# Block spectra of a long convolution: r's tiles ahead of u's, and x, v and decoded weights in other places

## The chip, the cores and the metric

The kernel runs on one core of one Trainium2 chip. The metric is the device time of one execution in microseconds.

## The reference

The inputs x and v are 12480 x 128, the positions 12480 x 64; everything is float32. A small network makes a filter from the positions, a long convolution mixes u = x * v with it, and two two-layer networks follow:

```
h_filt = (relu(pos_emb @ w1) @ w2) * exp(-0.01 * pos)
y = irfft(rfft(x * v, n=2*S) * rfft(h_filt, n=2*S))[:S]        # along the sequence, S = 12480
a = x * y
h = a @ w_in;  g = where(h > 0, h, exp(min(h, 0)) - 1);  b = g @ w_out          # d_ff = 2048
h = b @ w_in2; out = (max(h, 0) + alpha * min(h, 0)) @ w_out2
```

The weights of the two networks arrive with their 32-bit words interleaved in pairs as 64-bit numbers; the kernel decodes each of the four matrices into a rounded part (hi) and a remainder (lo).

## The kernel before

The Fourier transforms are block transforms, written as matrix products. The program is written out by hand in order: within an engine the order of the code is the order of the instructions, and engines wait for one another by semaphores. There are four stages.

The first makes r = relu(pos_emb @ w1): eight groups (`r_group`) of eight matmuls each, evicted from PSUM by ScalarE (one half) and VectorE (the other) into `rreg`, a buffer of 8192 columns per partition. Positions are loaded into the first 6272 columns of `ureg` (`load_pos`).

The second stage, the block spectra, has 48 tiles of four matmuls (`a_tile`), each into one of four PSUM buffers `pa` of two banks. The 16 r tiles (kind 1) multiply columns of `rreg` with `fw_sb` and are evicted into `sa` and `sb`; the 32 u tiles (kind 0) multiply u = x * v with `f_sb` and are evicted into `ureg`, which they fill altogether. ScalarE evicts the real half of each tile; VectorE evicts the other half in two tiles of three, ScalarE in the third. `order` lists two u tiles, then one r tile, sixteen times. `load_u` loads x and v of one u tile (98 partitions x 512 columns each, 0.40 MB for the pair) from SyncE's queue into a pool with five buffers for x and three for v; `mul_u` multiplies them, on GpSimd or on VectorE, into the buffer of x.

Beside this the weights are decoded. A piece is 512 columns of one matrix: `dec_load(j)` loads it (0.52 MB), and `dec_op(j, i)` is one of ten steps: 1 is ScalarE's absolute value, 2 to 6 are five VectorE operations (lines 112 to 120), 7 is ScalarE's cast to hi, 8 and 9 are GpSimd's subtraction and addition that make lo, and 10 writes hi and lo to memory (`wd`) for a later reload. Each piece needs a place of 2048 columns (`fixed`). `hooks` holds the steps that are issued after tile t. Pieces 0 to 2 are decoded in the r stage, 3 to 8 in the block spectra, 9 to 15 in the third stage. Pieces 0 to 2 are written from GpSimd's queue, 3 to 8 from ScalarE's, later ones from SyncE's; a queue's issue stands in the order of its engine's instructions.

The third stage is the spectrum loop over d = 0 to 24 (`b_r`, `b_u`, `b_h`, `products`, `z_mm`): products of the two spectra, with sums on GpSimd (lines 372 to 384), and their second transform, written to memory. b_r(0) starts when all tiles are evicted; its ScalarE copies go to `rt`, columns 7168 to 7680 of `rreg`. At its end `idle_mm` issues matmuls whose result nobody reads. The fourth stage is the two networks.

In an order listing DMAHWn and DMASWn are semaphores that count transfers issued by SyncE and ScalarE and by GpSimd; Pool, DVE, Activation and PE with a number are those of the engines.

Of the kernel before, what the change touches and what calls it, by code (L numbers as in the profile page):

```python
# [18 lines left out]
D = 128  # L19
P = 64  # L20
# [20 lines left out]
def kernel(ctx: ExitStack, tc: tile.TileContext, posT, w1b, w2b, sc2, xva, xT,  # L41
# [38 lines left out]
    ups = pb.enter_context(pool("ups", 4, side="right"))  # L80
# [15 lines left out]
    def dec_op(j, i):  # L96
# [26 lines left out]
        elif i == 8:  # L123
            nc.gpsimd.tensor_tensor(bf, bf, hi, ALU.subtract)
        elif i == 9:
            nc.gpsimd.tensor_tensor(lo, bf, a, ALU.add)
        elif nm in wd:
            (nc.gpsimd if j < 3 else nc.scalar if j < 9 else nc.sync).dma_start(wd[nm][:, :, k * 512 : (k + 1) * 512], rest.rearrange("p (x w) -> p x w", x=2))
# [24 lines left out]
    NU = D // 4  # L153

    def load_u(k, t=(0, 1)):
        for c in t:
            if k < NU:
                u_raw[k, c] = ups.tile([NI, 4, 2, P], F32, name="xv"[c], bufs=(5, 3)[c])
                nc.sync.dma_start(u_raw[k, c].rearrange("i c a p -> i (c a p)"),
                                  xva[:, c, 4 * k : 4 * k + 4].rearrange("i c a p -> i (c a p)"))  # L160

    def mul_u(k, eng=nc.gpsimd):
        u_done[k] = u_raw.pop((k, 0))
        eng.tensor_tensor(u_done[k], u_done[k], u_raw.pop((k, 1)), ALU.mult)
# [20 lines left out]
    w1_sb = col(NG * GW + 4096, 128)  # L185
# [4 lines left out]
    for j in range(3):  # L190
        fixed[j] = halves(col(NG * GW + 2048 * j, 2048) if j < 2 else dreg)
    dec_load(0)
    load_pos(2, 2)
    dec_load(1)
    load_pos(4, 2)
    nc.sync.dma_start(f_sb, fmat)
    load_u(0)
    load_pos(6, 2)
    load_u(1)
    load_pos(8, 2)  # L200
    dec_load(2)
    load_pos(10, 2)
    load_u(2)
    load_pos(12, 2)
    load_pos(14, 2)
    load_u(3)
    load_u(4)
    nc.sync.dma_start(fw_sb[:NI, : 2 * NF], fwin)
    nc.sync.dma_start(w2_sb, w2b)
    load_u(5, (1,))  # L210
    hooks = {3: [(mul_u, (0,))], 4: [(mul_u, (1,))], 6: [(mul_u, (2, nc.vector))]}
    for j, s in enumerate((0, 1, 4)):
# [6 lines left out]
    mul_u(3, nc.vector)  # L219

# [22 lines left out]
    order = []  # L243
    for k in range(CC // 4):
        order += [(0, 2 * k), (0, 2 * k + 1), (1, k)]
    order = order[:-3] + [order[-1]] + order[-3:-1]

    rfree = [halves(rreg[:, 2048 * x : 2048 * x + 2048]) for x in range(2)]
    fixed.update({9: rfree[1], 3: halves(dreg), 4: rfree[0], 5: halves(dreg), 6: rfree[1], 7: rfree[0], 8: halves(dreg)})
# [610 lines left out]
```

## Time and profile before

| | us |
|---|---|
| median of 3 runs | 1418.32 (1416.62 to 1419.56) |
| the profiled execution | 1418.37 |
| its span | 1416.6 |
| TensorE busy | 1376.6 |
| VectorE busy | 1267.7 |
| ScalarE busy | 1080.5 |
| GpSimd busy | 946.0 |

The profile is one execution. Its times count from the start of the span; 1.8 us of the execution's own time lie around the span. TensorE is PE, VectorE DVE, ScalarE ACT, GpSimd POOL, SyncE SP; the queue of an engine has a q behind its name.

### The profile page before, as it was taken

Reading aid. Unit: us, or ns where it says so; the run is one execution under the profiler, and the core shown is the slowest. Engines: PE = TensorE matmul, PEld = TensorE weight load, DVE = VectorE, ACT = ScalarE, POOL = GpSimd, SP = SyncE. Lnnn points to the kernel's source line nnn. Section 1 sums busy time; section 2 is a strip of 40 time slices with the busy share of each in tenths; the row PEclk is TensorE's granted clock in tenths of the full one; section 3 lists DMA queues with packets and bytes.
Section 4 is the critical chain, followed back from the end, with each engine's and each line's share of the span. In section 5 each row is a group of like instructions: output and inputs, shape, how many; then the busy total and the mean of one; then the engine's idle time right before and its main releaser. Section 6 shows DMA issues by size and latency. Waiting matters only on the chain.

```text
span 1416.6 us, 27103 instructions
## 1 busy us (share of the span) xinstructions
PE 1376.6 (97%) x10133; PEld 1171.5 (83%) x10133; DVE 1267.7 (89%) x1782; ACT 1080.5 (76%) x2041; POOL 946.0 (67%) x840
## 2 busy tenths in 40 slices
PE   6978999899999999999999999999999999999998
PEld 6977777688888888888888888888888888888897
DVE  5677999899999999999999999999999999999997
ACT  3545676588888788888888888887888888888884
POOL 4575788666666666666676666766667666666666
PEclk9999999999999999999999999999999999999999
DMA  8785776830010000000005000000000000000000
GB/s 268 229 256 174 215 236 195 234 106 25 29 55 26 27 26 8 19 26 26 19 8 209 26 26 19 8 26 26 25 19 8 26 26 26 19 8 23 8 8 14
DMA packets 56923, 97.61 MB, mean 69 GB/s; under 512 B 4506, under 2 KB 37432, under 8 KB 55366
## 3 DMA queue, kind: packets, MB, share of 16 engines
q1 hardware_dynamic: 53276, 84.75, 19.8%
q0 software_dynamic: 1568, 7.90, 1.9%
q10 hardware_dynamic: 1947, 3.22, 0.6%
q8 instruction: 80, 1.31, 0.4%
q14 instruction: 52, 0.43, 0.1%
HBM read 70.13 MB, written 25.66 MB: 68 GB/s over the span
## 4 chain that ended last, share of the span: by engine, by line
PE 86%; DVE 6%; DMA 3%; issue 2%; ACT 1%; POOL 1%; SPq 0%; POOLq 0%; ACTq 0%; DVEq 0%
PE psh L587 13%; PE pso L588 13%; PE psh L588 13%; PE pso L589 13%; PE pso L587 13%; PE psh L589 12%; PE psi L486 3%; PE pa L225 3%; DMA x<-in_xva_dram 2%; DVE spreg L355 2%; DMA ureg<-in_posT_dram 1%; PE pu L327 1%; PE pzz L393 1%; PE prh L337 1%; PE prh L307 1%
## 5 line engine op out<-in xcount | busy, mean ns | idle before, releaser
L610 POOL TENSOR_TENSOR g1l<-ureg,g1h 128x486 fp32r<-128x486 f32 (+3 forms) x313 | 364.3, 1164 | 201.7 <-ACT g1h L636 197.9
L610 POOL TENSOR_TENSOR g2l<-ureg,g2h 128x490 fp32r<-128x490 f32 (+3 forms) x315 | 346.4, 1100 | 121.6 <-ACT g2h L659 45.7
L648 DVE TENSOR_SCALAR ureg<-psh,al_sb 128x486 f32<-128x486 f32 (+3 forms) x416 | 296.0, 712 | 53.3 <-PE psh L589 52.9
L622 ACT ACTIVATE ureg<-psh 128x490 f32<-128x490 f32 (+2 forms) x393 | 225.9, 575 | 90.4 <-PE psh L589 87.3
L653 DVE SCALAR_TENSOR_TENSOR ureg<-psh,ureg 128x486 f32<-128x486 f32 (+3 forms) x416 | 274.1, 659 | 14.3
L630 DVE SCALAR_TENSOR_TENSOR ureg<-ureg,psh 128x486 f32<-128x486 f32 (+3 forms) x416 | 268.4, 645 | 4.2 <-ACT ureg L623 2.6
L636 ACT CAST g1h<-ureg 128x490 fp32r<-128x490 f32 (+3 forms) x405 | 240.0, 593 | 19.5 <-DVE ureg L630 18.6
L623 ACT ACTIVATE ureg<-ureg 128x490 f32<-128x490 f32 (+2 forms) x393 | 239.8, 610 | 12.5
L659 ACT CAST g2h<-ureg 128x490 fp32r<-128x490 f32 (+3 forms) x404 | 234.8, 581 | 8.7 <-DVE ureg L653 6.4
L587 PE MATMUL psh<-sb,sa 128*128 128x486 f32 (+3 forms) x416 | 160.8, 386 | 0.2 <-ACT sb L490 0.2
L588 PE MATMUL psh<-sb,sa 128*128 128x486 f32 (+3 forms) x416 | 158.9, 382 | 1.2 <-DVE sb L491 1.2
L587 PE MATMUL psh<-x2h,sb 128*128 128x486 f32 (+3 forms) x416 | 158.6, 381 | 1.1 <-ACT x2h L679 1.1
L588 PE MATMUL psh<-x2l,sb 128*128 128x486 f32 (+3 forms) x416 | 158.7, 382 | 0.4 <-DVE x2l L680 0.4
L589 PE MATMUL psh<-x2h,wc 128*128 128x486 f32 (+3 forms) x416 | 158.3, 381 | 0.0
L589 PE MATMUL psh<-sb,sa 128*128 128x486 f32 (+3 forms) x416 | 157.3, 378 | 0.0
L588 PE MATMUL pso<-g1l,sa 128*128 128x490 f32 (+3 forms) x405 | 155.4, 384 | 0.7 <-POOL g1l L610 0.4
L588 PE MATMUL pso<-g2l,wc 128*128 128x490 f32 (+3 forms) x404 | 155.5, 385 | 0.5 <-POOL g2l L610 0.5
L589 PE MATMUL pso<-g2h,wc 128*128 128x490 f32 (+3 forms) x404 | 154.9, 383 | 0.0
L587 PE MATMUL pso<-g1h,sa 128*128 128x490 f32 (+3 forms) x405 | 154.4, 381 | 0.0
L589 PE MATMUL pso<-g1h,sb 128*128 128x490 f32 (+3 forms) x405 | 154.4, 381 | 0.0
L587 PE MATMUL pso<-g2h,wc 128*128 128x490 f32 (+3 forms) x404 | 154.2, 382 | 0.0
L610 DVE TENSOR_TENSOR g1l<-ureg,g1h 128x490 fp32r<-128x490 f32 (+3 forms) x104 | 122.2, 1175 | 14.6 <-ACT g1h L636 3.7
(135 smaller groups left out, 2383.6 us busy)
## 6 DMA issues: line engine op xcount, KB each, us to landing
rreg<-in_gmat_dram SPq DMA_DIRECT2D x24, 384.0 KB
ureg<-in_finv_dram SPq DMA_DIRECT2D x24, 379.0 KB
ureg<-zhi SPq DMA_DIRECT2D x4, 1584.0 KB
x<-in_xva_dram SPq DMA_DIRECT2D x32, 196.0 KB
v<-in_xva_dram SPq DMA_DIRECT2D x32, 196.0 KB
zlo<-rreg SPq DMA_DIRECT2D x24, 256.0 KB
zhi<-rreg SPq DMA_DIRECT2D x22, 256.0 KB
ureg<-zlo SPq DMA_DIRECT2D x2, 1980.0 KB
```

Source lines behind the costliest of these rows:

```text
L225: nc.tensor.matmul(ps[:, 256 * e : 256 * e + 2 * NF], src[:, c0 + e].rearrange("i a p -> i (a p)"), fm, start=True, stop=True)
L587: nc.tensor.matmul(ps[:, :w], ah, bh[:, :w], start=start, stop=False)
L588: nc.tensor.matmul(ps[:, :w], ah, bl[:, :w], start=False, stop=False)
L589: nc.tensor.matmul(ps[:, :w], al, bh[:, :w], start=False, stop=stop)
L610: eng.tensor_tensor(lo[:, :w], e[:, :w], hi[:, :w], ALU.subtract)
L622: nc.scalar.activation(e[:, :w], ps[:, :w], AF.Relu, scale=-1.0)
L623: nc.scalar.activation(e[:, :w], e[:, :w], AF.Exp, scale=-1.0)
L630: nc.vector.scalar_tensor_tensor(e[:, :w], e[:, :w], -1.0, ps[:, :w], op0=ALU.add, op1=ALU.max)
L636: nc.scalar.copy(hi[:, :w], e[:, :w])
L648: nc.vector.tensor_scalar(e[:, :w], ps[:, :w], 0.0, al_sb[:, c : c + 1], op0=ALU.min, op1=ALU.mult)
L653: nc.vector.scalar_tensor_tensor(e[:, :w], ps[:, :w], 0.0, e[:, :w], op0=ALU.max, op1=ALU.add)
L659: nc.scalar.copy(hi[:, :w], e[:, :w])
```

## The change

The 16 r tiles come first and the 32 u tiles after them. The pool for x and v becomes a list of places: eight of 512 columns in a new buffer `ring`, and, once r tile k is multiplied, column block k of `rreg`, except blocks 4 to 7 and 11 to 14, which serve as places for pieces 6, 9 and 8. A v place comes free with its product, an x place with its tile. `load_u` loads as many pairs as there are places; in the r stage two pairs are loaded one at a time between pieces, and one after w2, and the positions come ahead of most other loads. Pieces 0 to 3 and 5 are decoded in columns of `ureg` behind the positions; pieces 2, 3, 5 and 4 move so that loads come in the r stage and steps from tile 2, 4, 7 and 12 on. Writes of pieces 3 to 8 are issued from GpSimd. A quarter of the products is on VectorE. In the spectrum loop two idle matmuls go, and the last two steps of piece 15 move from behind the loop into it.

```diff
@@ -77,7 +77,7 @@
     f_sb = fpool.tile([NI, 2 * NF], F32, name="f_sb")
     dreg = fpool.tile([128, 2048], F32, name="dreg")
     sc_sb = fpool.tile([128, 1], F32, name="sc_sb")
-    ups = pb.enter_context(pool("ups", 4, side="right"))
+    ring = fpool.tile([128, 4096], F32, name="ring")
     psa = pb.enter_context(pool("psa", 4, space=PSUM))
 
 
@@ -125,7 +125,7 @@
         elif i == 9:
             nc.gpsimd.tensor_tensor(lo, bf, a, ALU.add)
         elif nm in wd:
-            (nc.gpsimd if j < 3 else nc.scalar if j < 9 else nc.sync).dma_start(wd[nm][:, :, k * 512 : (k + 1) * 512], rest.rearrange("p (x w) -> p x w", x=2))
+            (nc.gpsimd if j < 9 else nc.sync).dma_start(wd[nm][:, :, k * 512 : (k + 1) * 512], rest.rearrange("p (x w) -> p x w", x=2))
 
     DV = (9,)
     pieces = [(src, nm, k) for src, nm in ((wo2, "wo2"), (wi2, "wi2"), (wo1, "wo1"), (wi1, "wi1")) for k in range(4)]
@@ -151,17 +151,27 @@
 
     u_raw, u_done = {}, {}
     NU = D // 4
-
-    def load_u(k, t=(0, 1)):
-        for c in t:
-            if k < NU:
-                u_raw[k, c] = ups.tile([NI, 4, 2, P], F32, name="xv"[c], bufs=(5, 3)[c])
-                nc.sync.dma_start(u_raw[k, c].rearrange("i c a p -> i (c a p)"),
-                                  xva[:, c, 4 * k : 4 * k + 4].rearrange("i c a p -> i (c a p)"))
+    free = [(ring[:, 512 * x : 512 * x + 512], False) for x in range(8)]
+    nload = [0]
+
+    def load_u(most=99):
+        while most and len(free) >= 2 and nload[0] < NU:
+            k = nload[0]
+            for c in range(2):
+                u_raw[k, c] = free.pop(0)
+                nc.sync.dma_start(u_raw[k, c][0][:NI], xva[:, c, 4 * k : 4 * k + 4].rearrange("i c a p -> i (c a p)"))
+            nload[0] += 1
+            most -= 1
+
+    def release(place):
+        if not (place[1] and nload[0] > NU - 10):
+            free.append(place)
 
     def mul_u(k, eng=nc.gpsimd):
-        u_done[k] = u_raw.pop((k, 0))
-        eng.tensor_tensor(u_done[k], u_done[k], u_raw.pop((k, 1)), ALU.mult)
+        x, v = u_raw.pop((k, 0)), u_raw.pop((k, 1))
+        eng.tensor_tensor(x[0][:NI], x[0][:NI], v[0][:NI], ALU.mult)
+        release(v)
+        u_done[k] = x
 
     NG = P // PH
     GW = PH * NI
@@ -182,42 +192,42 @@
             else:
                 nc.scalar.activation(dst, src, AF.Relu)
 
-    w1_sb = col(NG * GW + 4096, 128)
+    w1_sb = col(NF * 2 * D - 128, 128)
     nc.scalar.dma_start(w1_sb, w1b)
     load_pos(0)
     nc.scalar.dma_start(sc_sb, sc2)
     load_pos(1)
-    for j in range(3):
-        fixed[j] = halves(col(NG * GW + 2048 * j, 2048) if j < 2 else dreg)
+    rfree = rreg[:, 2048:4096]
+    fixed.update({j: halves(col(NG * GW + 2048 * j, 2048)) for j in range(4)})
+    fixed.update({4: halves(dreg), 5: halves(col(NG * GW + 8192, 2048)), 6: halves(rfree), 7: halves(dreg), 8: halves(rreg[:, 5632:7680]), 9: halves(rfree)})
+    load_pos(2, 2)
     dec_load(0)
-    load_pos(2, 2)
+    load_pos(4, 2)
+    load_pos(6, 2)
     dec_load(1)
-    load_pos(4, 2)
-    nc.sync.dma_start(f_sb, fmat)
-    load_u(0)
-    load_pos(6, 2)
-    load_u(1)
     load_pos(8, 2)
-    dec_load(2)
     load_pos(10, 2)
-    load_u(2)
     load_pos(12, 2)
     load_pos(14, 2)
-    load_u(3)
-    load_u(4)
     nc.sync.dma_start(fw_sb[:NI, : 2 * NF], fwin)
+    dec_load(2)
+    load_u(1)
+    dec_load(3)
+    nc.sync.dma_start(f_sb, fmat)
+    load_u(1)
+    dec_load(5)
     nc.sync.dma_start(w2_sb, w2b)
-    load_u(5, (1,))
-    hooks = {3: [(mul_u, (0,))], 4: [(mul_u, (1,))], 6: [(mul_u, (2, nc.vector))]}
-    for j, s in enumerate((0, 1, 4)):
+    load_u(1)
+    dec_load(4)
+    load_u()
+    hooks = {}
+    for j, s in enumerate((1, 4)):
         for i, d in enumerate((0, 0, 0, 0, 0, 0, 1, 1, 1, 2), 1):
             hooks.setdefault(s + d, []).append((dec_op, (j, i)))
     for g in range(NG // 2):
         run_hooks(hooks, g)
         r_group(g)
     run_hooks(hooks, 99)
-    mul_u(3, nc.vector)
-
 
     def a_tile(src, c0, fm, dsts, d0, shared, scale=None, cuts=(0, NF)):
         ps = psa.tile([128, 1024], F32, name="pa")
@@ -240,15 +250,16 @@
                 else:
                     nc.scalar.activation(o, x, AF.Copy, scale=scale)
 
-    order = []
-    for k in range(CC // 4):
-        order += [(0, 2 * k), (0, 2 * k + 1), (1, k)]
-    order = order[:-3] + [order[-1]] + order[-3:-1]
-
-    rfree = [halves(rreg[:, 2048 * x : 2048 * x + 2048]) for x in range(2)]
-    fixed.update({9: rfree[1], 3: halves(dreg), 4: rfree[0], 5: halves(dreg), 6: rfree[1], 7: rfree[0], 8: halves(dreg)})
-    hooks = dec_plan({3: 1, 4: 12, 5: 17, 6: 24, 7: 28, 8: 33}, (4, 5, 5, 6, 7, 7, 9, 10, 12, 14))
-    hooks.setdefault(40, []).append((dec_load, (9,)))
+    order = [(1, k) for k in range(CC // 4)] + [(0, k) for k in range(NU)]
+    hooks = {}
+    for j, load, s in ((2, None, 2), (3, None, 4), (5, None, 7), (4, None, 12), (6, 14, 19), (7, 22, 27), (8, 28, 33), (9, 40, None)):
+        if load is not None:
+            hooks.setdefault(load, []).append((dec_load, (j,)))
+        if s is not None:
+            for i, d in enumerate((0, 1, 1, 2, 3, 3, 5, 6, 7, 8), 1):
+                hooks.setdefault(s + d, []).append((dec_op, (j, i)))
+    for k in range(NU):
+        hooks.setdefault((5, 7, 9, 10)[k] if k < 4 else (13 if k % 4 == 3 else 11) + k, []).append((mul_u, (k, nc.vector if k % 4 == 3 else nc.gpsimd)))
     gts = {}
 
     def load_g(d):
@@ -260,15 +271,17 @@
     for t, (kind, k) in enumerate(order):
         if kind:
             a_tile(r_sb, 4 * k, fw_sb[:NI, : 2 * NF], a_rs, 4 * k, t % 3 != 0, scale=sc_sb, cuts=(0, NR, NF))
-            if k == 11 or k == 13:
-                load_g(k // 13)
+            if not (3 < k < 8 or 10 < k < 15):
+                free.append((rreg[:, 512 * k : 512 * k + 512], 7 < k < 11))
         else:
-            a_tile(u_done.pop(k), 0, f_sb, [a_u], 4 * k, t % 3 != 0, cuts=(0, 8, NF) if t == len(order) - 1 else (0, NF))
-            load_u(k + 5, (0,))
-            if 0 < k < NU - 3:
-                mul_u(k + 3, nc.vector if k % 6 == 2 else nc.gpsimd)
-            load_u(k + 6, (1,))
+            x = u_done.pop(k)
+            a_tile(x[0][:NI].rearrange("i (c a p) -> i c a p", c=4, a=2), 0, f_sb, [a_u], 4 * k, t % 3 != 0, cuts=(0, 8, NF) if t == len(order) - 1 else (0, NF))
+            release(x)
         run_hooks(hooks, t)
+        load_u()
+        if t == len(order) - 6:
+            load_g(0)
+    load_g(1)
     run_hooks(hooks, 99)
     nc.sync.dma_start(fw_sb, wmat)
     pb.close()
@@ -507,7 +520,7 @@
         when(s, dec_load, j)
         for i, d in ((2, 2), (3, 2), (4, 3), (5, 3), (6, 4)):
             mid.setdefault(t + d, []).append((j, i))
-        for i, d in ((1, 1), (7, 6), (8, 6), (9, 6), (10, 7))[: 5 if pieces[j][1] in wd else 2 if j == 15 else 4]:
+        for i, d in ((1, 1), (7, 6 - j // 15), (8, 6 - j // 15), (9, 6), (10, 7))[: 5 if pieces[j][1] in wd else 4]:
             when(t + d, dec_op, j, i)
     when(22, z_rows, 0, 80, 0, QA)
     when(24, z_rows, 80, 88, 0, QA)
@@ -549,11 +562,8 @@
     sums(nc.vector, nc.vector)
     writes.append(z_mm(ND - 3, (1,)))
     products(*late[1])(nc.gpsimd, nc.vector)
-    for i in (8, 9):
-        dec_op(15, i)
     idle_mm(pzz, FULL)
     writes.append(z_mm(ND - 2, (1,), prh))
-    idle_mm(pzz, FULL[:2])
     inv2(0)
     writes.append(z_mm(ND - 1, (1,), prh, 256))
     for write in writes:
```

On ScalarE, at the first u tile (`ureg<-pa`), before:

```order
L183 ACTIVATE rreg<-pa 98x2x64x4 [waits PE_49]
L122 CAST dreg<-dreg 128x512 [waits DVE_49]
L183 ACTIVATE rreg<-pa 98x2x64x4 [waits PE_49] x3
L239 COPY ureg<-pa 128x99x4 [waits DMAHW1_49,DMAHW0_49,DMAHW3_49,DMASW1_49,DMAHW4_49,DMASW0_49,DMAHW5_49,PE_49,DMAHW6_49,Activation_49,Pool_49]
L239 COPY ureg<-pa 128x99x4
L239 COPY ureg<-pa 128x99x4 [waits PE_49]
```

and in the changed kernel, where DMASW0 to DMASW4 count the writes of pieces 0, 1, 2, 3 and 5:

```order
L251 ACTIVATE sb<-pa,sc_sb 128x49x4
L251 ACTIVATE sa<-pa,sc_sb 128x50x4
L251 ACTIVATE sb<-pa,sc_sb 128x49x4
L249 COPY ureg<-pa 128x99x4 [waits DMASW3_49,DMASW4_49,DMASW2_49,DMAHW2_49,DMASW1_49,DMAHW3_49,DMASW0_49,DMAHW4_49,PE_49,DMAHW7_49,Activation_49,Pool_49]
L249 COPY ureg<-pa 128x99x4 [waits PE_49]
L122 CAST dreg<-dreg 128x512 [waits DVE_49]
L249 COPY ureg<-pa 128x99x4 [waits PE_49]
```

The first copy of a u tile stood behind the last r group and waited for two writes; now it stands behind the 16 r tiles, waits for five, and the cast of piece 4 (`dreg`) stands behind it.

On GpSimd, in the same stretch, before (`x<-x,v` is a product, `wd` a write to memory):

```order
L164 TENSOR_TENSOR x<-x,v 98x512 [waits DMAHW2_49,DMAHW1_49]
L128 DMA wd_wo_62<-ureg 256x1x512 [waits Pool_49]
L164 TENSOR_TENSOR x<-x,v 98x512 [waits DMAHW5_49,DMAHW4_49]
L124 TENSOR_TENSOR dreg<-dreg 128x512 [waits Activation_49]
L126 TENSOR_TENSOR dreg<-dreg 128x512 [waits DMAHW7_49,DVE_49,Pool_49]
L128 DMA wd_wo_62<-dreg 256x1x512 [waits Pool_49]
L164 TENSOR_TENSOR x<-x,v 98x512 [waits DMAHW7_49,DMAHW0_49]
```

and in the changed kernel:

```order
L124 TENSOR_TENSOR ureg<-ureg 128x512 [waits Activation_49]
L126 TENSOR_TENSOR ureg<-ureg 128x512 [waits DMAHW1_49,DVE_49,Pool_49]
L128 DMA wd_wo_62<-ureg 256x1x512 [waits Pool_49]
L124 TENSOR_TENSOR ureg<-ureg 128x512 [waits Activation_49]
L126 TENSOR_TENSOR ureg<-ureg 128x512 [waits DMAHW5_49,DVE_49,Pool_49]
L128 DMA wd_wi_61<-ureg 256x1x512 [waits Pool_49]
L172 TENSOR_TENSOR rreg<-rreg 98x512 [waits DMAHW5_49,DMAHW4_49,PE_49]
L172 TENSOR_TENSOR rreg<-rreg 98x512 [waits DMAHW7_49,DMAHW6_49,PE_49]
L172 TENSOR_TENSOR ring<-ring 98x512 [waits DMAHW1_49,DMAHW0_49]
L124 TENSOR_TENSOR dreg<-dreg 128x512 [waits Activation_49]
L126 TENSOR_TENSOR dreg<-dreg 128x512 [waits DVE_49,Pool_49]
L172 TENSOR_TENSOR ring<-ring,rreg 98x512 [waits DMAHW5_49,DMAHW4_49]
```

Where one piece stood between products there are now the steps and writes of pieces 3, 5 and 4 (`dreg`), and piece 4's first step stands ahead of eighteen of the products.

On GpSimd at the end of the spectrum loop of the changed kernel (L385, L396 and L397 are the sums, lines 372, 383 and 384 before):

```order
L124 TENSOR_TENSOR ureg<-ureg,sa 128x512 [waits Activation_49]
L385 TENSOR_TENSOR spreg<-spreg,rreg 128x2x256 [waits DVE_49]
L396 TENSOR_TENSOR rreg<-spreg 128x2x2x128 [waits DVE_49,PE_49,Pool_49]
L397 TENSOR_TENSOR rreg<-spreg 128x2x2x128 [waits PE_49]
L126 TENSOR_TENSOR sa<-ureg 128x512 [waits DMAHW2_49]
L396 TENSOR_TENSOR rreg<-spreg 128x256 [waits DVE_49,PE_49]
L397 TENSOR_TENSOR rreg<-spreg 128x256 [waits PE_49]
```

The steps L124 and L126 of piece 15 stood behind the last sum; they now stand ahead of the sums of iteration 22 and between those of 22 and 23.

## Rows read from the trace of the kernel before

**Rows 1.** Busy time by stage, four stretches; (x) is the number of instructions.

```profile
core 0: us, PE busy (x) PEld busy (x) DVE busy (x) ACT busy (x) POOL busy (x), PEclk, DMA share, GB/s
0.00:29.60 29.60, 17.29 (x129) 15.96 (x130) 16.44 (x23) 8.68 (x14) 12.27 (x14) 1.00 0.92 273
29.60:57.80 28.20, 28.18 (x169) 27.88 (x167) 13.87 (x25) 14.33 (x34) 14.67 (x12) 1.00 0.72 220
57.80:109.50 51.70, 41.93 (x220) 39.25 (x224) 39.53 (x58) 24.87 (x60) 33.99 (x25) 0.93 0.82 247
...
112.20:257.10 144.90, 137.77 (x3559) 109.09 (x3559) 132.97 (x167) 93.17 (x182) 112.82 (x92) 1.00 0.69 200
```

**Rows 2.** Chain that ended last, in order of time: start us, us, what.

```profile
53.09 7.15 DMA x<-in_xva_dram
```

**Rows 3.** Timeline of TensorE: start us, us, instructions, [idle before, releaser].

```profile
3.68 3.73 PE L175 MATMUL pa<-ureg 128*98 128x128 f32 x16 [3.68 <-DMA ureg<-in_w1b_dram]
...
25.94 3.71 PE L175 MATMUL pa<-ureg 128*98 128x128 f32 x32 [1.12 <-DMA ureg<-in_posT_dram]
29.48 2.85 PE L225 MATMUL pa<-f_sb,x 98*128 98x198 f32 x16
...
56.28 1.50 PE L225 MATMUL pa<-fw_sb,rreg 98*128 98x198 f32 x8
...
106.65 2.84 PE L225 MATMUL pa<-f_sb,x 98*128 98x198 f32 x16
```

**Rows 4.** Waits between 29.6 and 109.5 us: in total, times, longest.

```profile
SPq L159 <- POOL x L164: 33.0, 19, 3.7
...
POOL x L164 <- DMA x<-in_xva_dram: 18.8, 9, 4.1
```

**Rows 5.** Groups by line, 29.6 to 109.5 us, VectorE and ScalarE.

```profile
L237 DVE TENSOR_SCALAR sa<-pa,sc_sb 128x200 f32<-128x200 f32 x15 | 6.3, 421 | 12.5 <-ACT sb L241 12.3
L237 DVE TENSOR_SCALAR sb<-pa,sc_sb 128x196 f32<-128x196 f32 x15 | 6.2, 411 | 0.0
...
L241 ACT ACTIVATE sa<-pa,sc_sb 128x200 f32<-128x200 f32 x17 | 7.3, 431 | 5.8 <-PE pa L225 4.5 <-POOL dreg L126 1.3
...
L122 ACT CAST rreg<-rreg 128x512 fp32r<-128x512 f32 x3 | 1.9, 622 | 4.6 <-DVE rreg L120 4.6
```

**Rows 6.** VectorE in single pieces' decoding, alone, then on dreg (DVE first).

```profile
8.46:11.19 2.73, 2.58 (x5) 1.00 1.04 312
...
21.20:25.56 4.36, 4.20 (x5) 1.00 0.97 297
...
95.60:104.40 8.80, 6.78 (x5) 0.00 (x0) 0.00 (x0) 0.81 0.97 302
```

**Rows 7.** Landing of GpSimd's three writes, line 128, 0 to 40 us.

```profile
DMA to landing us min/median/max: 4.1/7.9/8.0
```

**Rows 8.** Timeline of GpSimd: two products (L164) and the write issues (L128).

```profile
15.01 0.84 POOL L128 DMA_DIRECT2D wd_wo<-ureg  x1 [0.31 <-POOL ureg L126]
...
20.23 1.27 POOL L164 TENSOR_TENSOR x<-x,v 98x512 f32<-98x512 f32 x1
...
29.65 0.68 POOL L128 DMA_DIRECT2D wd_wo<-dreg  x1 [0.30 <-POOL dreg L126]
...
69.82 1.71 POOL L164 TENSOR_TENSOR x<-x,v 98x512 f32<-98x512 f32 x1
```

**Rows 9.** Timeline of ScalarE: the first copies into rt (L312).

```profile
110.59 1.54 ACT L312 COPY rreg<-prh 64x256 f32<-64x256 f32 x4 [0.51 <-PE prh L307]
```

**Rows 10.** Timeline of TensorE at the end of the spectrum loop.

```profile
256.43 0.73 PE L425 MATMUL pzz<-sa 128*128 128x512 f32 x2
257.09 1.58 PE L486 MATMUL pu<-ureg 99*64 99x98 f32 x32
```

**Rows 11.** Timeline of GpSimd at the end of the spectrum loop.

```profile
244.97 1.28 POOL L383 TENSOR_TENSOR rreg<-spreg 128x512 f32<-128x512 f32 x1 [0.57 <-DVE spreg L379]
...
247.45 0.72 POOL L383 TENSOR_TENSOR rreg<-spreg 128x256 f32<-128x256 f32 x1
```

## The prediction

> **What bounds the kernel now.** I first read the busy times by stage [rows 1]. From 112.2 us on, in the spectrum loop and then in the two MLPs, TensorE is busy 95% and more; the change hardly touches that part. What it rebuilds is the time before: 29.6 us in which r is made, then the block spectra. In the first 28.2 us of the spectra TensorE is busy all the time (28.18 of 28.20). In the next 51.7 us it is busy 41.93, with a granted clock of 0.93, and the transfers run at 0.82 of their engines and 247 GB/s: this stretch is where time can be had. The chain of waits there is led by an x load that takes 7 us to land [rows 2]. By the TensorE timeline [rows 3] the last positions end their wait at 25.94 us, one r group at full pace is 3.71 / 2 = 1.86 us, and from 29.48 to 57.78 us 21 tiles pass, 28.3 / 21 = 1.34 us each. The last tile pair begins at 106.65 and ends at 109.49 us. So 48 tiles at full pace would be 64.3 us, and the stage takes 80.0. Who starves it: SyncE's queue waited 33.0 us for GpSimd's products, because a v load needs one of only three v buffers back, and GpSimd in turn waited 18.8 us for x [rows 4]. The loop load, product, release goes round at the length of a load, while the transfers are not full.
>
> **The change, part by part.** Durations are from the profiled execution: span 1416.6, its own time 1418.37 us, which is the median of the runs (1418.32) within 0.05.
>
> *Order of loads in the r stage.* Before, 6.07 MB stand in SyncE's queue up to the last positions (3.21 positions, three pieces of 0.52, three x and v pairs of 0.40, fmat); after, 4.26 MB (positions and two pieces). The last positions came at 25.94 [rows 3]; in proportion, with the first issue some 0.7 us after the start (an estimate), they land at 18.4. TensorE alone needs 3.68 + 8 x 1.86 = 18.6 [rows 3]. I take the last group at 18.7 and its end at 20.6, against 29.65 before. The gain of 9 us is not kept whole: before, u tiles filled TensorE while the last r group was evicted. Now the first r tile needs that eviction, two passes in a row, which I put at 0.7 each from the 0.42 to 0.43 of a copy of a tile [rows 5] and the waits between: r tiles start at 22.0.
>
> *r's 16 tiles first.* At pace they end at 22.0 + 21.4 = 43.4. VectorE has the odd rows of two tiles in three, 0.421 + 0.411 = 0.83 us each [rows 5], and now three pieces (2, 3, 5) besides. A piece's five VectorE operations cost 2.58 us where GpSimd stood still and 4.20 and 6.78 where it worked [rows 6]. GpSimd will work here about as in the 4.20 row, so I take 4.5. Start at tile 1's end, 22.0 + 2.68 + 0.86 (ScalarE's half) = 25.5; seven such evictions (5.8) and three pieces (13.5) stand before piece 5's last operation: 44.8.
>
> *The new wait.* Pieces 0 to 3 and 5 now stand in the columns into which the u tiles are evicted. Hence the first u eviction, on ScalarE and on VectorE, waits until GpSimd has written piece 5 to memory. Before, it waited for pieces 0 and 1 alone, written long before. Piece 5: VectorE done 44.8, ScalarE's cast 0.62 [rows 5] makes 45.4, two GpSimd operations of 1.36 (33.99 us / 25, [rows 1]) and 0.3 make 48.4. The write's landing is known from three: 4.1, 7.9, 8.0 us [rows 7]. I take the middle of the ends, L = 6.0: u evictions start at 54.4. TensorE can fill four buffers meanwhile (to 48.8) and then stands. Behind the blocked ScalarE copy stands the cast of piece 4, behind that in GpSimd's queue all further products.
>
> *GpSimd as the pace.* Two copies and the cast (1.6) later GpSimd has 18 products, 8 decode operations and 4 write issues in front of tile 30: 26 x 1.36 = 35.4, and 4 x 0.73 = 2.9 [rows 8]. Tiles 30 and 31 add 2.7. The last tile ends at 54.4 + 1.6 + 35.4 + 2.9 + 2.7 = 97.0. TensorE's own pace from 54.4 is shorter: 0.9 + 28 x 1.34 = 38.4, to 92.8. The 16 places hold 13 pairs by then; the transfers still need the other 19 (7.6 MB), two pieces (1.05) and three writes (1.57), which at the 302 GB/s of a full stretch [rows 6] is 34 us, also shorter. Bounds: GpSimd operations at the 1.27 of an undisturbed product [rows 8] take 2.3 off, at the 1.71 of a disturbed one add 9.1; L from 4.1 to 8.0.
>
> *Writes from GpSimd.* Six issues leave ScalarE's queue, where they were hidden (ScalarE is busy 24.87 of 51.7, [rows 1]), and four of them are the 2.9 above. Piece 8's write now gates the spectrum loop: its place holds rt, so ScalarE's first copy of b_r(0) waits for it. It is issued 1.4 + 0.7 before product 30 ends and needed 5.9 us after the issue: with L = 6.0 a wait of 0.1, up to 2.1 with 8.0. Before, that copy came 1.1 us after the last tile [rows 9], counted in the same 5.9.
>
> *The end of the spectrum loop.* Two idle matmuls go, 0.66 us between their start and the next group [rows 10]. Piece 15's two GpSimd operations move into iterations 22 and 23. There GpSimd has 0.57 us of slack before the sums of iteration 22 and none after [rows 11]; 1.27 + 1.29 us therefore put the sums of iteration 23 some 2 us later, and what TensorE and the row transfers need from iteration 24 about 1.1. I take +1.1 - 0.66 = +0.4, with -0.66 and +2 as bounds.
>
> *Sum.* 97.0 - 109.49 = -12.5; +0.1; +0.4: **-12.0**, so 1418.37 - 12.0 = **1406.4 us**.
>
> The Trainium skill speaks against the writes: its page "SBUF — State Buffer", section "Summary: rules for kernel authors", says to issue from ScalarE or SyncE a transfer that is to hide under VectorE work, since GpSimd's descriptor generation starves while VectorE uses the shared port. The trace agrees in part: two of the three landings were 7.9 and 8.0 us, but in stretches full of loads, and issue took only 0.68 to 0.84. The page's example (620 ns alone, 3100 overlapped) gives an estimate of 2.5 us more per write, twice on the path, and 1411.4 us; the first rival below is the same case worked out from rows.
>
> **The rivals.**
>
> *The writes come late (slower).* One mechanism at two gates: with landing L the last tile ends at 91.0 + L, and rt waits L - 5.9 more. The sum is L - 18.5 + 0.4 + (L - 5.9): zero at L = 12.0, and slower by 0.2% from 13.4. At twice the longest row, 16, it is +8.0: 1426.4. For it: two of three landed at the long end, and loads will be queued deeper. Against: 4.1 where fewer were. Chance 0.10.
>
> *The wait is hidden and TensorE sets the pace.* With a piece at 2.58 on VectorE, piece 5 is done at 39.0 and written, with 4.1, at 46.7, before the four buffers are full. With GpSimd at 1.27 the last tile ends at 46.7 + 1.6 + 33.0 + 2.9 + 2.7 = 86.9, TensorE's own 22.0 + 64.3 = 86.3: -22.6 + 0.4 = 1396.2. For it: the first half before ran at full pace with all this traffic. Against: VectorE's 4.20 to 6.78 [rows 6]. Chance 0.20, with half-way cases to 1401.
>
> *The transfers are the bound, and the change does little.* Up to 109.5 us 273 x 29.6 + 220 x 28.2 + 247 x 51.7 = 27.0 MB moved [rows 1]; no transfer is dropped. At the mean of 247 GB/s the stage ends where it ended, 1415 to 1420. For it: the shares of 0.92 and 0.82. Against: 302 and 312 GB/s in full stretches [rows 6], and the 33.0 us for which the queue waited on buffers [rows 4], which 16 places for x and v remove. Chance 0.12.
>
> *GpSimd at 1.71 an operation:* 97.0 + 9.1, so 1415.5. Chance 0.10.
>
> **How the numbers follow.** The forecast, with 0.48, has its own range of 1402 to 1411 (L, GpSimd's price down to 1.27, the loop's end, and the clock: 0.93 over 51.7 us is worth 3.6 us, which I neither credit nor charge). 1397 to 1417 leaves out the late writes (0.10), the lower half of the hidden case and a few of the transfer case, less than 0.2. A measurement here tells about 0.2% (2.8 us) from no change: faster, below 1415.5, is 0.48 + 0.20 + half of the 1.71 case and a little of the transfer case, 0.76; slower is 0.10; the rest, 0.14, is within.
>
> **What would show it.** r tiles from 22 us and u tiles right after; ScalarE's first u copy ended by a transfer of the decoded weights, at 50 to 57; then GpSimd busy over 90% until the last tile at 94 to 100, with few waits for x; SyncE waiting less than half of 33.0 us for GpSimd; rt's first copy within 2 us of the last tile; iteration 23's sums later against iteration 22's by about 1.3. Wrong would be: u evictions without a stop (hidden case), SyncE's loads still landing after 7 us with GpSimd idle on x (transfer case), or landings over 10 us of what GpSimd writes (late writes).

## The result and the profile after

The changed kernel takes 1426.63 us (median of 4 runs, 1425.06 to 1427.57) against 1417.47 for the kernel before (4 runs): a ratio of 1.0063, 95% interval 1.0048 to 1.0078. It is slower by 0.6%, where 1406.4 was forecast. The profiled execution takes 1425.06, with a span of 1423.0 us, 6.4 more than before.

The stages first, as in [rows 1]:

```profile
core 0: us, PE busy (x) PEld busy (x) DVE busy (x) ACT busy (x) POOL busy (x), PEclk, DMA share, GB/s
0.00:29.60 29.60, 24.43 (x173) 24.00 (x174) 13.42 (x24) 13.54 (x28) 9.43 (x12) 1.00 0.94 305
29.60:57.80 28.20, 22.66 (x128) 21.56 (x127) 25.47 (x38) 17.28 (x45) 17.57 (x15) 0.97 0.70 221
57.80:109.50 51.70, 39.43 (x190) 38.61 (x189) 35.18 (x37) 16.95 (x37) 33.59 (x29) 0.82 0.74 221
```

The r stage is done early: in the first 29.6 us TensorE is busy 24.43 instead of 17.29. From 57.8 on it is busy 39.43 of 51.7 at a granted clock of 0.82 (41.93 and 0.93 before), and the transfers fall from 247 to 221 GB/s: they are not the bound. TensorE's timeline, which answers to [rows 3], says where the time is lost:

```profile
3.65 16.93 PE L185 MATMUL pa<-ureg 128*98 128x128 f32 x128 [3.65 <-DMA ureg<-in_w1b_dram]
22.00 19.34 PE L235 MATMUL pa<-fw_sb,rreg 98*128 98x198 f32 x112 [1.41 <-DVE rreg L191]
43.92 2.92 PE L235 MATMUL pa<-fw_sb,rreg 98*128 98x198 f32 x16 [2.59 <-DVE sb L247]
...
55.32 4.60 PE L235 MATMUL pa<-f_sb,rreg 98*128 98x198 f32 x16 [2.62 <-DVE ureg L245]
...
65.87 2.98 PE L235 MATMUL pa<-f_sb,rreg 98*128 98x198 f32 x8 [4.61 <-DVE rreg L172]
...
82.29 1.68 PE L235 MATMUL pa<-f_sb,rreg 98*128 98x198 f32 x8 [3.44 <-DVE rreg L172]
...
99.15 5.36 PE L235 MATMUL pa<-f_sb,ring 98*128 98x198 f32 x16 [4.22 <-ACT rreg L122]
...
112.39 1.50 PE L235 MATMUL pa<-f_sb,ring 98*128 98x198 f32 x8
```

The r tiles begin at 22.00. Then there are stops of 2.59 (VectorE's evictions of r tiles), 2.62 (the gate of the first u eviction), 4.61, 3.44 and 4.22 us, the third and fourth ended by a product of VectorE (`rreg`, L172); the fifth is put down to ScalarE's cast, but the tile at 99.15 needs VectorE's product at 98.32, so it is of the same kind. The last tile ends at 112.39 + 1.50 = 113.89, against 109.49 before. VectorE's timeline from 49 us on, its four longest operations and one product:

```profile
49.56 3.95 DVE L116 SCALAR_TENSOR_TENSOR dreg<-dreg 128x512 uint32<-128x512 uint32 x1
...
59.61 5.52 DVE L114 TENSOR_SCALAR rreg<-rreg 128x512 uint32<-128x512 uint32 x1
65.05 0.68 DVE L172 TENSOR_TENSOR rreg<-rreg 98x512 f32<-98x512 f32 x1
...
77.22 3.86 DVE L112 TENSOR_SCALAR dreg<-dreg 128x512 f32<-128x512 f32 x1
...
93.08 4.13 DVE L116 SCALAR_TENSOR_TENSOR rreg<-rreg 128x512 uint32<-128x512 uint32 x1
```

L112, L114 and L116 are decoding steps that take 0.4 to 0.7 us where GpSimd stands still. Here they take 3.86 to 5.52, and the product at 65.05, for which TensorE has stood since 61.26, stands right behind the longest. GpSimd's timeline at that place:

```profile
59.23 0.67 POOL L128 DMA_DIRECT2D wd_wi<-dreg  x1
59.86 1.33 POOL L172 TENSOR_TENSOR ring<-ring,rreg 98x512 f32<-98x512 f32 x1
61.09 1.31 POOL L172 TENSOR_TENSOR rreg<-rreg,ring 98x512 f32<-98x512 f32 x1
62.31 1.30 POOL L172 TENSOR_TENSOR ring<-ring 98x512 f32<-98x512 f32 x1
63.53 1.30 POOL L172 TENSOR_TENSOR ring<-ring,rreg 98x512 f32<-98x512 f32 x1
72.32 1.27 POOL L124 TENSOR_TENSOR rreg<-rreg 128x512 f32<-128x512 f32 x1 [7.49 <-ACT rreg L122]
```

At 59.23 GpSimd issues a write (L128); from 59.86 to 64.83 it computes four products without a gap. VectorE's step began inside the issue, at 59.61, and ended at 65.13, 0.3 us after the run. The other three long steps read the same way: each began 0.2 to 0.4 us after a write issue had ended (48.53 + 0.68, 76.37 + 0.68, 92.24 + 0.68) and ended 0.3 to 0.6 us after GpSimd's run of products. The last row shows what comes back to GpSimd: it stood 7.49 us until ScalarE's cast of that piece.

```profile
71.61 0.63 ACT L122 CAST rreg<-rreg 128x512 fp32r<-128x512 f32 x1
```

VectorE's last step for this cast had ended at 67.86; the cast stood in ScalarE's queue behind evictions of tiles that TensorE, held up by the product, made late. Over all, behind the gate:

```profile
POOL rreg L124 <- ACT rreg L122: 10.0, 2, 7.5
POOL dreg L124 <- ACT dreg L122: 4.6, 2, 2.5
```

After the stop at 61.26 TensorE ran at half its clock until about 70 (0.50 is the lower of its two levels):

```profile
64.00:67.00 3.00, 1.13 (x4) 1.16 (x5) 3.00 (x5) 0.00 (x0) 0.83 (x1) 0.50 0.11 16
67.00:70.00 3.00, 3.00 (x11) 3.00 (x10) 1.43 (x4) 0.49 (x1) 0.00 (x0) 0.50 0.90 290
70.00:73.00 3.00, 3.00 (x20) 3.00 (x19) 0.86 (x2) 1.83 (x4) 0.68 (x1) 1.00 0.86 255
```

Of the 6.4 us, 4.4 are there when the last tile ends; the rest comes in the spectrum loop. Its last full iteration takes 9.01 us, from ScalarE's copies into `rt` to its next copy from `prh`, against 7.09 before (ScalarE after, then before):

```profile
246.82 1.54 ACT L325 COPY rreg<-prh 64x256 f32<-64x256 f32 x4 [1.16 <-PE prh L320]
...
255.83 0.58 ACT L417 COPY rreg<-prh 128x512 f32<-128x512 f32 x1 [2.15 <-PE prh L406]
```

```profile
242.72 1.54 ACT L312 COPY rreg<-prh 64x256 f32<-64x256 f32 x4 [1.25 <-PE prh L307]
...
249.81 0.59 ACT L404 COPY rreg<-prh 128x512 f32<-128x512 f32 x1 [0.23 <-PE prh L393]
```

The two moved steps L124 and L126 stand there (GpSimd's rows, to be read against [rows 11]); experiment 4 asks whether the 1.9 us are theirs:

```profile
247.15 1.27 POOL L124 TENSOR_TENSOR ureg<-ureg,sa 128x512 f32<-128x512 f32 x1
...
252.20 1.30 POOL L126 TENSOR_TENSOR sa<-ureg 128x512 fp32r<-128x512 f32 x1
```

### The profile page after: what moved, and what is told of

The parts are those of the page before. It is cut to its first block, busy times and chain, and to the rows that moved or that the text cites. A ratio compares the mean times of both kernels' runs of the same rounds, so it can differ in the third digit from the quotient of the medians.

```text
span 1423.0 us, 27055 instructions
## 1 busy us (share of the span) xinstructions
PE 1381.8 (97%) x10131; PEld 1178.4 (83%) x10131; DVE 1273.7 (90%) x1778; ACT 1082.0 (76%) x2046; POOL 946.2 (66%) x845
## 4 chain that ended last, share of the span: by engine, by line
PE 86%; DMA 1%; DVE 1%; POOL 1%; issue 1%; ACT 1%; POOLq 0%; ACTq 0%; SPq 0%
PE psh L597 13%; PE pso L598 13%; PE pso L599 13%; PE psh L598 12%; PE pso L597 12%; PE psh L599 12%; PE psi L499 3%; PE pzz L406 2%; PE pu L340 2%; PE prh L350 2%; PE prh L320 1%; DMA wc<-wd_wo 1%; DVE spreg L368 0%; ACT rreg L325 0%; POOL rreg L397 0%
```

## The experiments

The first theory (A) was that GpSimd, computing without a gap, stretches VectorE's decoding steps, and that the products behind them are late; its rivals were the writes from GpSimd (B), the gate of the first u eviction (C) and a VectorE that is simply full (D). Each kernel was timed in three rounds beside the kernel before, whose median was 1417.3 to 1418.4 in these rounds. "rt" is the start of ScalarE's first copy into `rt`, the end of the stage; "longest" is VectorE's longest operation from 45 us to there that does not read PSUM.

| kernel | median us | ratio to before (95%) | rt us | longest us |
|---|---|---|---|---|
| before | 1417.5 | 1 | 110.59 | 2.52 |
| changed | 1426.6 | 1.0063 (1.0048 to 1.0078) | 115.03 | 5.52 |
| 1 writes from ScalarE | 1422.5 | 1.0034 (1.0018 to 1.0050) | 110.01 | 2.67 |
| 2 products on VectorE | 1415.4 | 0.9994 (0.9973 to 1.0015) | 103.47 | 1.77 |
| 3 piece 5 in the ring | 1429.0 | 1.0079 (1.0048 to 1.0110) | 116.68 | 5.91 |
| 4 old end of the loop | 1425.9 | 1.0055 (1.0036 to 1.0075) | 117.64 | 5.91 |
| 5 both 1 and 2 | 1416.9 | 0.9994 (0.9977 to 1.0012) | 103.67 | 1.78 |
| 6 VectorE's products early | 1419.2 | 1.0015 (1.0006 to 1.0024) | 108.78 | 5.93 |
| 7 steps left out | 1413.4 | 0.9973 (0.9961 to 0.9986) | 104.12 | 7.78 |
| 8 before, writes from GpSimd | 1418.4 | 1.0006 (0.9997 to 1.0016) | 108.43 | 2.58 |
| 9 both, fewer evictions, old end | 1417.3 | 0.9988 (0.9976 to 1.0000) | 106.10 | 1.77 |
| 10 early, ScalarE writes, old end | 1416.6 | 0.9994 (0.9982 to 1.0006) | 107.73 | 1.76 |
| 11 as 9 with half on GpSimd | 1418.4 | 1.0004 (0.9990 to 1.0018) | 108.21 | 2.99 |
| 12 before, products on VectorE | 1415.5 | 0.9981 (0.9966 to 0.9996) | 102.61 | 1.56 |

**1. Writes from ScalarE.**

```diff
-            (nc.gpsimd if j < 9 else nc.sync).dma_start(wd[nm]...
+            (nc.gpsimd if j < 3 else nc.scalar if j < 9 else nc.sync).dma_start(wd[nm]...
```

> The changed kernel (1426.6) with one part undone: the writes of pieces 3 to 8 are issued from ScalarE's queue again. Theory A (VectorE starved: a decoding step on VectorE that meets GpSimd computing without a gap lasts until the gap, 5.52 us in place of 0.43 in the worst case; VectorE's products stand behind it and TensorE waits for them, 4.61, 3.44 and 4.22 us, and comes back at half its clock): the products stay as they are, so within 2 us, 1424.5 to 1428.5, and the three waits of TensorE for VectorE's products stay. Theory B (the writes from GpSimd come late, or hold GpSimd up): at least 5 us back, 1421.5 or less. The first u eviction should end its wait at 52.5 or up to 0.7 earlier, since one issue of 0.68 leaves GpSimd ahead of it.

Neither theory had the size: 4.1 us came back. The first u eviction ended its wait at 53.73, later than the 52.5 that was expected. VectorE's timeline at the place of the longest step, and GpSimd's:

```profile
57.84 1.50 DVE L112 TENSOR_SCALAR rreg<-rreg 128x512 f32<-128x512 f32 x1
59.38 1.38 DVE L114 TENSOR_SCALAR rreg<-rreg 128x512 uint32<-128x512 uint32 x1
60.68 1.75 DVE L172 TENSOR_TENSOR rreg<-rreg 98x512 f32<-98x512 f32 x1
```

```profile
57.80 2.67 POOL L172 TENSOR_TENSOR ring<-ring,rreg 98x512 f32<-98x512 f32 x2
60.43 1.44 POOL L172 TENSOR_TENSOR rreg<-rreg,ring 98x512 f32<-98x512 f32 x1
61.84 2.32 POOL L172 TENSOR_TENSOR ring<-ring 98x512 f32<-98x512 f32 x1
```

GpSimd's run is as long as before, but without the issue ahead of it VectorE gets in between two operations: the steps take 1.38 to 1.50 and GpSimd's operations in turn up to 2.32. So the run alone does not shut VectorE out, and theory A had to be narrowed to A2: issue and run together.

**2. All products on VectorE.**

```diff
-        ...(5, 7, 9, 10)[k] if k < 4 else (13 if k % 4 == 3 else 11) + k, []).append((mul_u, (k, nc.vector if k % 4 == 3 else nc.gpsimd)))
+        ...(5, 7, 9, 10)[k] if k < 4 else 11 + k, []).append((mul_u, (k, nc.vector)))
```

> The changed kernel with one thing altered: all 32 products on VectorE instead of a quarter, each five tiles ahead of its tile. GpSimd keeps only the two operations of a piece and the writes. Theory A: VectorE's steps meet almost no GpSimd work and take 0.4 to 0.7 us each. After the first u eviction (52.5, unchanged) VectorE has 28 products of 0.68, 19 evictions of 0.57 and four pieces of 2.6, 40.3 us, against 37.5 of TensorE: the last tile ends at 93 to 98 instead of 113.9, and the kernel takes 1406 to 1412. Theory C (the gate: the wait of the first u eviction for piece 5's write is what costs): the gate stays, so 1423 to 1427. Theory D (VectorE is simply too full, and more work on it makes it worse): slower than 1428.

The stage ends 11.6 us earlier than in the changed kernel, and the median is 11.2 lower, less than the 15 to 20 that A gave: the last tile ends at 101.8, not at 93 to 98. The gate stays (the first u copy waits until 54.91) and VectorE has more to do, so theory D falls, and C is in doubt. The edit also brings VectorE's own quarter of the products two tiles forward, and experiment 6 shows that their place counts by itself. The issues are still GpSimd's; VectorE's rows, then GpSimd's:

```profile
58.20 1.77 DVE L172 TENSOR_TENSOR rreg<-rreg 98x512 f32<-98x512 f32 x1
...
60.38 0.67 DVE L172 TENSOR_TENSOR ring<-ring,rreg 98x512 f32<-98x512 f32 x1
```

```profile
57.81 1.61 POOL L126 TENSOR_TENSOR dreg<-dreg 128x512 fp32r<-128x512 f32 x1
59.72 0.68 POOL L128 DMA_DIRECT2D wd_wi<-dreg  x1 [0.30 <-POOL dreg L126]
```

Beside single GpSimd operations VectorE waits for one of them, 1.77 us; a product begun as the issue ends, with no run behind it, takes 0.67. Against the kernel before, 7.1 us at rt became about 2 in the median, and by the ratio nothing measurable. In the profiled run, itself one of the slower (1421.0), 4.0 us went back in the spectrum loop (150.5 us from rt to the inverse transform, 146.5 before), and the chain of waits shows one place behind it:

```profile
278.55 21.14 DMA wc<-wd_wo
```

TensorE stands 3.69 us there for weights that are read again (0.28 in the changed kernel). The single times run from 1413.0 to 1423.9, and this is one execution.

**3. Piece 5 in the ring.**

```diff
-    fixed.update({..., 5: halves(col(NG * GW + 8192, 2048)), ...
-    free = [... for x in range(8)]
+    fixed.update({..., 5: halves(ring[:, 2048:]), ...
+    free = [... for x in range(4)]
+    hooks[15].append((lambda: free.extend((ring[:, 512 * x : 512 * x + 512], False) for x in range(4, 8)), ()))
```

> The changed kernel with piece 5 decoded in the last four places of the ring, not in the columns of the u tiles; these four places serve x and v only after its write. The first u eviction then waits for pieces 0 to 3 alone, the last of them issued at 42.4: no wait at 48.5 instead of 3.9 us until 52.5. Theory C (the gate costs): all that follows comes 4 us earlier and TensorE's stop of 2.62 with the half clock after it (1.9) goes: 1422 or less. Theory A (VectorE starved by GpSimd's runs): the stops are where GpSimd's runs meet VectorE's steps, these stay, and at most 2 us come back: 1424.5 to 1428.

ScalarE's first u copy and, ahead of it, TensorE's last r tiles:

```profile
51.44 0.49 ACT L249 COPY ureg<-pa 128x396 f32<-128x396 f32 x1 [0.40 <-ACT sb L251]
```

```profile
44.01 5.62 PE L235 MATMUL pa<-fw_sb,rreg 98*128 98x198 f32 x16 [2.58 <-DVE sb L247]
```

The gate is gone, and nothing is gained (1429.0): the copy comes at 51.44, because here TensorE ran two r tiles in 5.62 us, at half its clock, after its stop at 41.4. The long operations stand where they stood, the longest of them now a product (L172, 5.91 us at 59.82). The edit also leaves fewer places for early loads, but no stop of TensorE in this stage is put down to a load. Theory C falls as the main cause.

**4. The old end of the loop.**

```diff
-        for i, d in ((1, 1), (7, 6 - j // 15), (8, 6 - j // 15), (9, 6), (10, 7))[: 5 if ... else 4]:
+        for i, d in ((1, 1), (7, 6), (8, 6), (9, 6), (10, 7))[: 5 if ... else 2 if j == 15 else 4]:
+    for i in (8, 9):
+        dec_op(15, i)
     idle_mm(pzz, FULL)
     writes.append(z_mm(ND - 2, (1,), prh))
+    idle_mm(pzz, FULL[:2])
```

> The changed kernel with the end of the spectrum loop as before: the last two steps of piece 15 behind the loop, and the two idle matmuls. From the first copy into rt to the start of the inverse transform it takes 148.3 us in the changed kernel and 146.5 before. If the moved steps on GpSimd are the 1.8 us: 146.5 again and 1424.8 in all. If the loop is longer for another reason (loads or reads moved, the half clock): 148 and more, 1426 to 1427.

The last full iteration takes 7.09 us again, but 149.1 from rt to the inverse transform, since single stops elsewhere in the loop differ from run to run. The time does not differ measurably. In the profiles with the moved steps that iteration took 7.33 to 9.01, in those without them 7.08 to 7.96, so how much of the 1.9 us is theirs is not shown.

**5. Both 1 and 2.**

> Both earlier edits at once: all products on VectorE, and the writes of pieces 3 to 8 from ScalarE. Theory A2 (VectorE is shut out only where GpSimd issues a write and then computes several operations without a gap; such a step lasts to the end of that run, 3.86 to 5.91 us in three runs so far, and never over 1.9 where either the issue or the run is missing): with the products on VectorE nothing is left to gain from the writes, 1413 to 1417, as with the products alone (1415.4). Theory B2 (each write from GpSimd costs by itself, 4.1 us in all as the first experiment gave back): the two add up, 1409 to 1412.

1416.9, as theory A2 has it: where there are no runs, the writes give nothing back. The bound of 1.9 us in the expectation was too low: run 1, with runs and without issues, had an operation of 2.67.

**6. VectorE's products early.**

```diff
-        ...(13 if k % 4 == 3 else 11) + k, []).append((mul_u, ...
+        ...(10 if k % 4 == 3 else 11) + k, []).insert(0 if k % 4 == 3 else 99, (mul_u, ...
```

> The changed kernel with only VectorE's eight products moved: three tiles earlier, and ahead of the decoding steps that are issued after the same tile. The writes stay on GpSimd, so VectorE's steps of 3.9 to 5.9 us stay. If the loss is that the product stands behind such a step and TensorE waits for it (4.61, 3.44 and 4.22 us, and some 7 us of half clock behind these stops), most of it comes back: last tile at 102 to 106, 1416 to 1420. If VectorE's evictions behind the long steps stop TensorE just as long, through its four PSUM buffers: 1424 to 1428.

7.4 us come back while the long operations stay: what was lost was mainly the product's place, too late and behind the step (the edit changes both). The longest VectorE operation is a product itself, as in 3 and 4, and a stop of TensorE remains, through the evictions:

```profile
60.54 5.93 DVE L172 TENSOR_TENSOR rreg<-rreg,ring 98x512 f32<-98x512 f32 x1
```

```profile
67.70 7.35 PE L235 MATMUL pa<-f_sb,rreg 98*128 98x198 f32 x24 [3.57 <-DVE ureg L245]
```

**7. Without VectorE's steps of pieces 4, 6, 7 and 8.**

```diff
     def dec_op(j, i):
+        if j in (4, 6, 7, 8) and 2 <= i <= 6:
+            return
```

> The changed kernel without the five VectorE steps of pieces 4, 6, 7 and 8, so that these pieces are not decoded (part of the weights is wrong; loads, casts, GpSimd's operations and writes stay). It gives what the stage takes if VectorE is never late. The prediction's own term for GpSimd as the pace (26 operations of 1.36, issues, two products behind the gate) then holds: last tile at 95 to 99, 1407 to 1412. If the loads or GpSimd are the bound in any case: last tile after 105, 1417 or more.

1413.4, the last tile at 102.1: between the two. VectorE had one long operation left, a product (L174 in this file), and rt waited for piece 8's write:

```profile
61.77 7.78 DVE L174 TENSOR_TENSOR rreg<-rreg,ring 98x512 f32<-98x512 f32 x1
```

```profile
104.12 1.54 ACT L327 COPY rreg<-prh 64x256 f32<-64x256 f32 x4 [1.46 <-DMA wd_wo<-rreg]
```

So a product is shut out as the steps are, for 7.78 us here; and the second gate of the prediction exists, at 1.46 us, once GpSimd and TensorE are on time. It shows in 6, 10 and 11 too (1.21, 1.14 and 1.69 us).

**8. The kernel before with the writes of pieces 3 to 8 from GpSimd** (the reverse of the first diff).

> The kernel before (1417.5) with one part of the change alone: the writes of pieces 3 to 8 from GpSimd. Theory B2 (a write from GpSimd costs by itself): 4 us slower, 1421 to 1423. Theory A2: there GpSimd computes with gaps, since it waits for x between products; few issues are followed by a run, so 1416 to 1420, with a step over 2.7 us only where two or more GpSimd operations follow an issue at once.

No measurable difference, as A2 expected, and not the 4 us of B2. The longest VectorE operation:

```profile
94.73 2.58 DVE L112 TENSOR_SCALAR dreg<-dreg 128x512 f32<-128x512 f32 x1
```

**9 to 11. Combinations.** 9 is 5 with one u eviction in three on VectorE (`t % 3 == 1` in place of `t % 3 != 0`) and the old end; 10 is 6 with the writes from ScalarE and the old end; 11 is 9 with products of even k on GpSimd.

> All products on VectorE, writes of pieces 3 to 8 from ScalarE, VectorE's share of the u evictions down from two tiles in three to one in three (ScalarE, busy 17 of 52 us there, takes the others), and the end of the spectrum loop as before. In the run with the first two edits alone TensorE stopped seven times for VectorE (0.2 to 0.7 us each, 3.2 in all). VectorE's work behind the gate falls from 51 to 45 us. If what VectorE has to do is now the bound: last tile at 98 to 101 in place of 102.5, and the end of the loop 0 to 1.9 us shorter, so 1411 to 1414.5. If the gain in this stage is taken back in the loop and behind it, as it was in part in the earlier run: 1415 to 1418.

> A quarter of the products on VectorE as in the changed kernel, but three tiles earlier and ahead of the decoding steps; the writes of pieces 3 to 8 from ScalarE; the end of the loop as before. GpSimd still computes runs of products, but no write is issued ahead of them. Theory A2 (only issue and run together shut VectorE out for a whole run): no VectorE operation over 2.8 us behind the gate, last tile at 100 to 105, 1412 to 1417. If the run alone does it when products stand in other places: steps of 4 us and more again, 1419 and up.

> As the kernel with all products on VectorE, few evictions, ScalarE writes and the old end, but with half of the products on GpSimd. If the two engines' operations take turns (each VectorE step beside a GpSimd operation lasts about as long as that, 1.3 to 1.4 us), GpSimd's products at 1.28 cost more of the shared time than VectorE's at 0.68, 14 of them 8 us more: last tile later than with all on VectorE, by 0 to 5 us, 1412 to 1418. If VectorE's own work was the bound and GpSimd's is free: earlier by 2 us or more.

In 9 the last tile ends at 99.9, and then TensorE stands for the first table of the loop:

```profile
104.06 1.99 PE L320 MATMUL prh<-rreg,sa 64*64 64x128 f32 x32 [4.13 <-DMA rreg<-in_gmat_dram]
```

4.13 us until a load lands. The chain of waits names what held the load:

```profile
92.01 8.58 DMA wd_wo<-rreg
100.65 3.27 DMA rreg<-in_gmat_dram
```

SyncE's queue stood 8.4 us and issued the load at 100.65; the profile puts that down to piece 8's write, issued at 92.01. No transfer ran from 99.5 to 101.5 us (DMA share 0.00), so the transfers are not the bound at this place. The gain in the stage is taken back, as the second expectation had it. 10 has no operation over 1.76 us behind the gate, with runs and without issues. In 11 the last tile ends at 105.5, 5.6 us later than in 9, as if operations of the two engines took turns; the times do not differ measurably.

**12. The kernel before with the products on VectorE.**

```diff
-                mul_u(k + 3, nc.vector if k % 6 == 2 else nc.gpsimd)
+                mul_u(k + 3, nc.vector)
```

> The kernel before with all products from the fifth on VectorE, nothing else: does the gain of the products on VectorE need the changed order and places? If it does not: 1411 to 1415. If loads that wait for one of three v places are the bound there: 1416 to 1419. If VectorE waiting in order for a load holds up its evictions: 1420 or more.

0.9981 (0.9966 to 0.9996): of the versions that compute everything the only one whose interval lies below 1, by little and one among eleven, and it has nothing of the change in it. The median lies between the first two expectations. TensorE from the first tile to the last, to be read against [rows 1]:

```profile
27.00:101.40 74.40, 68.68 (x386) 65.38 (x384) 57.24 (x108) 38.57 (x93) 20.61 (x15) 0.98 0.83 257
```

## Why the prediction was wrong

- **Order of loads, r tiles first: right.** r's matmuls end at 3.65 + 16.93 = 20.58 (forecast 20.6), the r tiles begin at 22.00 (22.0). They end at 46.7, not at 43.4: TensorE stopped 2.59 us for evictions that stood behind a step of 2.77 us on VectorE, a loss that the gate covered.
- **The new wait: right, with the landing mis-sized.** VectorE finished piece 5 at 44.84 (44.8), in part by luck: its three pieces took 2.6, 4.1 and 6.0 us, not 4.5 each. The write was issued at 48.53 (48.4), and ScalarE's first u copy started at 52.50 (54.4); the write took 3.6 us to land, not 6.0. The profile puts this wait down to a load that landed last; in run 2 the same wait is put down to the write.

```profile
52.50 0.88 ACT L249 COPY ureg<-pa 128x396 f32<-128x396 f32 x2 [3.90 <-DMA rreg<-in_xva_dram]
```

- **GpSimd as the pace: this step failed.** It added up GpSimd's own work behind the gate, and the price was right: 26 operations of 1.33 us (26 of 1.36). But GpSimd was not the pace. It stood 14.6 us for four casts, two of which waited for VectorE's last step (54.73 and 98.44) and two behind evictions of late tiles (71.61 and 87.03), and TensorE stood 4.61, 3.44 and 4.22 us for products that VectorE had not come to. With the measured gate the forecast's terms give 95.1; the last tile ended at 113.9. From 55.32 on 28 tiles at pace are 37.5 us, and 58.6 passed: 12.3 in the three stops, most of the other 8.8 at half clock. I had used VectorE's stretched prices (4.20, 6.78) only up to piece 5, and left VectorE out of everything after it, though its products and evictions stand in one queue with those steps. Run 6 shows the order, runs 1, 2 and 10 the shutting out.
- **Writes from GpSimd: hidden in their own time, not in what they do to VectorE.** Each issue of pieces 3 to 8 took 0.65 to 0.68 us. The cost was that VectorE, meeting an issue and then a run, waits for the whole run; 1 against the changed kernel, 5 against 2, and 8 show that both are needed.
- **The late writes.** That rival's worked time, 1426.4, is what was measured, by chance: at its first gate the write landed after 3.6 us. At its second, piece 8's write took 10.7 us, more than the 10 that were named as a sign of this rival, but rt was not kept waiting, since the last tile came later still. In the variants whose last tile comes earlier (6, 7, 9, 10, 11) that write does hold the loop up, in 9 by way of a load.
- **The transfers.** Not the bound in the changed kernel (221 GB/s). In 9 they ran at 277 GB/s from 57.8 to 99.9, and the last tile ended 9.6 us before that of the kernel before, so the mean of 247 that this rival rested on was no limit.
- **The end of the loop.** Forecast +0.4 with +2 as bound: 1.9 in the profile, of which the share of the moved steps is not shown, and not measurable in the times (4).
- **The clock,** neither credited nor charged: 0.82 against 0.93. It was a cost, most of the 8.8 us above, behind the stops.
- **The chances.** "Less than 0.2" outside the range does not follow from its own parts: 0.10, half of 0.20 and a few of the transfer case are over 0.2.

The Trainium skill, page "SBUF — State Buffer", section "Summary: rules for kernel authors", also says that a VectorE operation with two SBUF inputs, or in its faster two-port mode, and a GpSimd operation on SBUF cannot run together: the later one waits until the earlier has finished. Run 1 agrees in size (1.38 to 1.50 for steps of 0.4), though no run shows in which mode these steps ran. The changed kernel differs: behind an issue VectorE waited for three or four operations, 3.86 to 5.52 us. The Trainium skill's advice in the same section, to issue from ScalarE or SyncE a transfer that is to hide under VectorE work, held, 4.1 us here. But what waited was VectorE: issuing a write took GpSimd 0.65 to 0.68 us, and the write at the gate landed in 3.6 us.

**Open:** why an issue ahead of a run keeps VectorE out at the boundaries between GpSimd's operations, where it otherwise gets in. The runs show that it does, not how. Also open is why the rest of the stage's gain is lost in 2, 5 and 9. Their profiles show where most of it goes: the loop takes 150.5, 152.4 and 150.0 us from rt to the inverse transform, 146.5 before; but its stops differ from run to run.

## What to carry to other kernels

When loads come early enough that an engine no longer waits, look at what its waits were giving to others: here VectorE got on with its work on SBUF in GpSimd's gaps. Add up a stage for each engine that stands in the chain with the prices that hold beside a busy neighbour, and follow in each queue what stands behind the stretched operation. A product that takes 0.68 us on VectorE and 1.3 us on GpSimd is not free on GpSimd: a VectorE step beside it took 1.38 to 1.50 us instead of 0.4, and moving all products to VectorE gave the stage 11.6 us back.

## What was not expected of the hardware

In the changed kernel and runs 3, 4, 6 and 7, a VectorE operation on SBUF that began inside a GpSimd write issue, or in the run of GpSimd operations directly behind one, with at least one operation of the run still to come, lasted to the end of that run: 2.46 to 7.78 us (in 7 it began 1.4 us after the issue had ended). There are exceptions: steps that began 0.02 us into an issue took 0.43, and in run 3 a step got in ahead of the run's fourth operation, after 3.86 us. From 45 us to rt, such operations took at most 2.99 us in every kernel that had only runs, issues with at most one operation behind them, or neither. And the same stop of 2.6 us at the end of the r tiles was followed by full clock in the changed kernel (two tiles in 2.92 us, granted 1.00) and by half clock in run 3 (5.62 us, granted 0.50).
